# A gated linear-attention kernel with an MLP behind it: gates of the last eight pairs loaded one token per partition, and a new order table on every engine

## The chip, the cores and the metric

One core of one Trainium2 chip runs the whole program. The metric is the device time of one execution in microseconds. The five engines are named as in the profile: PE (TensorE matmuls, with PEld for its weight loads), DVE (VectorE), ACT (ScalarE), POOL (GpSimd) and SP (SyncE, which here only issues DMAs). A "q" behind an engine's name (SPq, ACTq) is its sequencer.

## What is computed

Four batches, eight heads, 768 tokens, 48 channels per head. A complex gate decays a 48x48 state per head; the query reads it; the result of all heads (384 channels) goes through a layer norm and a two-layer MLP with a residual.

```python
mag = sqrt(a_re*a_re + a_im*a_im); scale = minimum(mag, 0.999) / (mag + 1e-06)
for t in range(S):                       # a_re, a_im scaled by `scale`
    S_re, S_im = (ar*S_re - ai*S_im) + k[t] v[t]^T,  ar*S_im + ai*S_re
    y[t] = q[t] @ S_re
x  = y, heads side by side               # (4, 768, 384)
xn = (x - mean) / sqrt(var + 1e-06) * g_ln
out = x + maximum(xn @ w_ch1, 0) @ w_ch2     # 384 -> 1536 -> 384
```

## The kernel before

The 768 tokens of a batch are cut into six chunks of 128, and two chunks make a pair: 12 pairs, P = 0 to 11, chunk n = 2P + c with c = 0 or 1. All work of a pair is made of named steps.

- Loads: `are.P`, `aim.P` (the two parts of the gate), `k.P.c`, `q.P.c`, `vf.P.c`. Each tile has a small ring of buffers (`are`, `aim`, `q`, `k` three, `vf` two), and a load waits until its buffer is free. A gate load of a pair is one DMA of 384 KB: partition p holds the two neighbouring tokens 2p and 2p+1, so that a run of 384 bytes is contiguous in memory (line 445). `k`, `q` and `vf` are loaded one token per partition, in runs of 192 bytes (line 404). Pair 0 is worked in two halves of four heads (`PARTS`), its steps end in `.0.0` and `.0.1`.
- Gate, on ACT, DVE and POOL: `ln` (w = ln a_re), `iv` (1/a_re), `r` = a_im/a_re, `r2`, `u` = ln(1 + r2), `l` and `lc` (log of the magnitude, capped), `th` = arctan r.
- Sums over tokens, on PE: `dec` (line 477) adds up the logs with triangular matrices `u_e`, `ph` (492 and 496) adds up the angles with `u_th` and takes over the carry of the pair before (`car`, through `pick`). Since a partition holds two tokens, each of the two chunks needs the products of both: four 384-column products for `dec`, and four and two with `pick` for `ph`.
- `e`, `en` (exponentials), `sin`, `cos` (with `abs`, or for pairs 0 to 2 a quarter turn `qt`), then `ke`, `qe` (k and q with their decays) and `ks`, `qs` (times cosine and sine).
- Attention within the chunk: `ksT`, `qsT` (transposed by PE as `kT`/`qT` and a copy, or by a DMA from SP), `am` (products), `atm` (mask), `gm` and `G` (state), `y`, `x`. `v` is `vf` in bf16. `dps`, `decc`: the pair's whole decay.
- MLP: `xtr`, `xT` (transposed x), `bn`, `rstd` (layer norm), `mm1` with `relu` (hidden layer, three groups `.P.g` of two parts), `mm2` with `oa` and `ot` (output), `st` (store).
- `warm.i` are fill-ins: products of 256 columns whose result nobody reads, 134 of them, all before the first product of the MLP. `wl` load the weights, `wp` and `wc` fold the layer norm into them. `tab` loads a table of functions on ACT.

The order is written out by hand in one table, `PLAN`: each entry names a step, its engine (P, A, V, G for POOL, S) and, where it needs one, its PSUM bank. Every engine works through its own entries in that order and waits for what a step needs. A load or store with S is issued by SP, one with A by ACT, between ACT's other work. `@name` makes a step wait for the step named, so that POOL and DVE take turns. Which engine does a step is thus decided in the table: `ks:V` on DVE, `ks:G` on POOL.

Of the kernel before, what the change touches and what calls it, by code (L numbers as in the profile page):

```python
# [34 lines left out]

ENGINES = {"P": "PE", "A": "ACT", "V": "DVE", "G": "POOL", "S": "SP"}
# [37 lines left out]
r2.4.0:V mm1.1.0.0:P4 th.4.0:A car.3.0:V0 mm2.0.0:P2 relu.1.0:A4 ke.2.0.1:V mm2.1.0:P3 qs.2.0.1:V vf.2.1:S cos.3.0:A
lc.3.0:V mm2.2.0:P4 qs.2.0.0:V bn.2:V tab.log.6:A qT.4:P5 mm2.1.1:P3 bn.1:V rstd.1:G dec.3.0:P0 ks.2.0.1:V u.4.0:A
ks.2.0.0:V mm2.0.1:P2 rstd.0:G en.3.0:A0 l.4.0:V ksT.5:S mm2.2.1:P4 e.3.0:A0 lc.4.0:V ln.5.0:A relu.1.2:V6
qe.3.0.1:G@lc.4.0 mm2.1.2:P3 qe.3.0.0:G mm2.0.2:P2 aim.5.0:S oa.1:A3 qT.5:P0 iv.5.0:A vf.3.0:A ot.0:V2 dec.4.0:P6
qsT.4:V5 mm2.2.2:P4 e.4.0:A6 vf.3.1:A qs.3.0.1:V kT.4:P1 qs.3.0.0:V en.4.0:A6 dps.3:P5 are.7.0:S dps.4:P2 ksT.4:V1
ke.3.0.0:G@qs.3.0.0 qT.6:P3 qsT.5:A0 ph.4.0:P6 ot.2:V4 aim.6.0:S ke.3.0.1:G ln.6.0:A decc.3:V5 decc.4:V2 am.4:P4
q.4.0:S v.2:G qsT.6:V3 mm2.3.0:P1 iv.6.0:A atm.4:V4 ks.3.0.1:G k.4.0:S qT.7:P2 tab.trig.7:A mm2.3.1:P1 qsT.7:V2  # L80
gm.4:P3 am.5:P4 sin.4.0:A6 ks.3.0.0:V k.4.1:S y.4:P2 atm.5:V4 r.5.0:G@ks.3.0.0 kT.6:P0 car.4.0:A6 mm2.3.2:P1 x.4:A2
G.4:A3 ksT.6:V0 k.5.1:S kT.7:P5 abs.4.0:A6 xtr.4:P4 ot.1:G y.5:P0 ksT.7:V5 q.4.1:S th.5.0:A am.6:P6 x.5:V0 v.3:G
k.5.0:S am.7:P2 xT.4:A4 atm.6:V6 xtr.5:P0 ph.5.0:P4 r2.5.0:G xT.5:A0 cos.4.0:A ot.3:V1 gm.6:P0 mm1.2.1.1:P6 atm.7:V2
G.6:A0 vf.4.1:A r.6.0:G aim.7.0:S abs.5.0:A4 y.6:P1 mm1.2.1.0:P6 x.6:V1 sin.5.0:A4 vf.4.0:A mm1.2.2.1:P2 relu.2.1:V6
cos.5.0:A xtr.6:P1 r2.6.0:G y.7:P4 mm1.2.2.0:P2 th.6.0:A st.0:A x.7:V4 gm.7:P0 bn.7:V xtr.7:P4 tab.log.8:A ke.4.0.1:G
mm1.2.0.0:P6 xT.6:V1 mm1.2.0.1:P6 q.5.1:S xT.7:V4 qe.4.0.0:G G.7:V0 u.5.0:A are.8.0:S mm1.3.0.1:P4 bn.6:V ke.4.0.0:G
mm1.3.0.0:P4 relu.2.2:A2 st.2:A relu.2.0:V6 qe.4.0.1:G mm1.3.1.1:P0 relu.3.0:A4 ks.4.0.0:V mm1.3.2.1:P2 rstd.3:G
ks.4.0.1:V u.6.0:A mm1.3.2.0:P2 l.5.0:V ksT.8:S mm2.5.0:P6 qs.4.0.1:V ln.7.0:A mm1.3.1.0:P0 lc.5.0:V q.5.0:S
qs.4.0.0:V kT.9:P7 relu.3.1:A0 l.6.0:V dec.5.0:P4 qsT.9:S mm2.5.1:P6 iv.7.0:A lc.6.0:V ksT.9:V7 mm2.6.0:P0 en.5.0:A4
q.6.0:S r.7.0:V mm2.4.0:P1 e.5.0:A4 qT.8:P7 q.7.0:S bn.5:V v.4:A r2.7.0:G@r.7.0 dec.6.0:P4 are.9.0:S bn.4:V  # L90
relu.3.2:A2 mm2.4.1:P1 k.6.0:S qsT.8:V7 mm2.6.1:P0 rstd.2:G en.6.0:A4 qe.5.0.1:V am.8:P2 ke.5.0.0:V e.6.0:A4
mm2.4.2:P1 qe.5.0.0:V ln.8.0:A atm.8:V2 gm.8:P7 ke.5.0.1:G@qe.5.0.0 q.6.1:S am.9:P4 iv.8.0:A mm2.6.2:P0 qe.6.0.0:G
atm.9:V4 u.7.0:A st.1:A mm2.5.2:P6 ph.6.0:P2 G.8:A7 vf.6.0:A ks.5.0.1:V k.6.1:S tab.trig.9:A qs.5.0.1:V mm2.7.0:P4
ot.4:V1 abs.6.0:V2 y.8:P5 th.7.0:A vf.5.1:A mm2.7.1:P4 l.7.0:V x.8:A5 vf.5.0:A gm.9:P7 y.9:P1 sin.6.0:A2 vf.6.1:A
mm2.7.2:P4 x.9:V1 car.6.0:A2 xtr.8:P5 qs.5.0.0:V xtr.9:P1 oa.7:A4 ph.7.0:P2 xT.9:V1 qsT.10:S ks.5.0.0:G@qs.5.0.0
xT.8:V5 cos.6.0:A ot.5:V6 qT.11:P1 G.9:V7 sin.7.0:A2 mm1.4.1.0:P4 qe.6.0.1:V abs.7.0:A2 st.4:A mm1.4.1.1:P4 ksT.10:S
qs.6.0.0:V mm1.4.0.1:P6 tab.log.10:A car.7.0:V2 ke.6.0.1:G@qs.6.0.0 mm1.4.0.0:P6 qsT.11:V1 mm1.4.2.0:P2 ln.9.0:A
# [116 lines left out]
def kernel(  # L214
# [12 lines left out]
    nc = tc.nc  # L227
# [596 lines left out]
```

## Time and profile before

| | |
|---|---|
| median of 3 runs | 191.19 us (191.16 to 192.15) |
| the profiled execution, its own time | 192.75 us |
| the profiled execution, span from first to last instruction | 191.0 us |
| instructions | 5154 |
| DMA packets, bytes | 133080, 37.57 MB |
| read from HBM, written | 28.31 MB, 4.72 MB |
| share of the chain that ended last | PE 63%, DVE 10%, ACT 9%, DMA 8%, issue 4% |

The page's busy shares are averages over the whole span; the view by windows gives them for a stretch of time. The mean time of one matmul in the groups holds its latency, since matmuls are pipelined; the time that one really takes of PE is the distance between starts, which the pieces of the chain show (so many products in so many microseconds). The "DMA share" of a window is the packets' time over that of 16 engines; packets of two queues overlap on an engine, so it can exceed 1.

### The profile page before, as it was taken

What the parts mean: (1) busy time and instruction counts of PE and PEld (TensorE: products, weight loads), DVE (VectorE), ACT (ScalarE), POOL (GpSimd) and SP (SyncE); (2) the same over time, 40 slices, a digit from 0 to 9 for tenths busy, and PEclk for the clock granted to TensorE, in tenths of its full rate; (3) what the DMA queues carried; (4) which work ended last, traced back from release to release, by engine and by line L of the source; (5) the groups of instructions that cost most, each with busy time, mean ns of one, the idle gap of its engine ahead of it and who ended that gap; (6) DMA issues with size and microseconds to landing.
All of it is one profiled execution on the core that took longest, in us unless ns stands there. A gap on an engine that the chain in (4) does not pass through costs nothing.

```text
span 191.0 us, 5154 instructions
## 1 busy us (share of the span) xinstructions
PE 177.3 (93%) x2045; PEld 138.6 (73%) x2045; DVE 156.6 (82%) x285; ACT 158.9 (83%) x224; POOL 105.5 (55%) x124
## 2 busy tenths in 40 slices
PE   5999398999999999999968999999999999998992
PEld 3888365788667887776847687877867777786781
DVE  1678699999999999999996998998989867666532
ACT  3989499999999997899949999998999979662340
POOL 7419032579196899071539483347785954940130
PEclk9999999999999999999999999999999999999998
DMA  6999999999969999889999999999799979994032
GB/s 153 278 240 202 212 198 204 210 214 207 242 108 287 205 220 234 154 183 234 136 265 234 190 221 230 282 223 204 141 160 262 217 126 179 256 191 151 5 124 82
DMA packets 133080, 37.57 MB, mean 197 GB/s; under 512 B 127168, under 2 KB 133056, under 8 KB 133056
## 3 DMA queue, kind: packets, MB, share of 16 engines
q1 hardware_dynamic: 107760, 27.21, 70.6%
q10 hardware_dynamic: 22512, 7.67, 18.0%
q0 software_dynamic: 2784, 2.36, 7.9%
q8 instruction: 16, 0.26, 0.6%
q14 instruction: 8, 0.07, 0.1%
HBM read 28.31 MB, written 4.72 MB: 173 GB/s over the span
## 4 chain that ended last, share of the span: by engine, by line
PE 63%; DVE 10%; ACT 9%; DMA 8%; issue 4%; ACTq 2%; POOL 1%; SPq 1%; DVEq 0%; POOLq 0%
PE banks L754 22%; PE banks L722 16%; PE banks L617 5%; PE banks L594 4%; DMA q<-in_q_dram 4%; DMA ksT<-ks 3%; PE banks L477 3%; PE banks L667 2%; ACTq L777 2%; PE banks L496 2%; PE banks L670 2%; DVE w1b L388 2%; DMA are<-in_a_re_dram 2%; PE banks L645 2%; PE banks L688 2%
## 5 line engine op out<-in xcount | busy, mean ns | idle before, releaser
L754 PE MATMUL banks<-w2b,h 128*128 128x384 bf16 (+1 forms) x300 | 55.7, 319 | 0.6 <-ACT h L739 0.6
L722 PE MATMUL banks<-xT,w1b 128*128 128x256 bf16 x432 | 50.9, 272 | 0.7 <-ACT h L739 0.5
L722 PEld LDWEIGHTS <-w1b 128*128 128x128 bf16 x432 | 41.4, 98 | 7.0 <-issue 1.2
L754 PEld LDWEIGHTS <-h 128*128 128x128 bf16 x300 | 26.7, 97 | 13.8 <-ACT h L739 1.0
L295 DVE TENSOR_TENSOR atm<-banks,mask 128x1024 bf16<-128x1024 f32 x24 | 29.0, 1219 | 3.8 <-PE banks L617 2.9
L739 ACT ACTIVATE h<-banks 128x1024 bf16<-128x1024 f32 (+1 forms) x26 | 25.7, 1009 | 4.6 <-DVE ks L295 2.6
L792 ACT ACT_TABLE_LOAD x19 | 24.4, 1283 | 2.6 <-PEq L808 1.3
L295 POOL TENSOR_TENSOR ke<-k,en 128x384 bf16<-128x384 f32 x17 | 15.4, 916 | 14.1 <-ACT e L481 4.3
L767 POOL TENSOR_TENSOR ot<-ot,x 128x384 f32<-128x384 f32 x13 | 12.5, 967 | 14.2 <-ACT ot L760 12.9
L295 POOL TENSOR_TENSOR r<-aim,are 128x768 f16<-128x768 f32 (+1 forms) x8 | 13.7, 1715 | 11.0 <-DVE w1b L388 4.1
L787 PE MATMUL banks<-u_e 128*128 128x256 f16 x134 | 17.5, 286 | 2.2 <-POOL u_e L323 2.2
L295 POOL TENSOR_TENSOR qs<-qe,trig 128x768 bf16<-128x768 bf16 x8 | 13.0, 1640 | 10.3 <-DVE w1b L388 7.2
L617 PE MATMUL banks<-qsT,ksT 128*128 128x128 bf16 x192 | 14.5, 219 | 2.8 <-ACT h L739 2.1
L787 PEld LDWEIGHTS <-u_e 128*128 128x128 f16 x134 | 13.5, 102 | 4.5 <-POOL u_e L323 1.9
L617 PEld LDWEIGHTS <-ksT 128*128 128x128 bf16 x192 | 12.1, 97 | 5.1 <-issue 2.8
L741 DVE TENSOR_SCALAR h<-banks 128x1024 bf16<-128x1024 f32 (+1 forms) x11 | 12.7, 1166 | 2.7 <-PE banks L722 2.7
L295 POOL TENSOR_TENSOR qe<-q,e 128x384 bf16<-128x384 f32 x12 | 11.0, 917 | 6.8 <-DVE r L295 3.6
L466 DVE SCALAR_TENSOR_TENSOR l<-r,w 128x768 f16<-128x768 f16 (+1 forms) x13 | 12.6, 969 | 1.3 <-ACT r L462 1.1
L680 DVE BATCH_NORM_STATS2 stats<-x 128x6 f32<-128x384 bf16 x24 | 13.1, 546 | 0.1
L667 PE MATMUL banks<-v,atm 128*128 128x48 bf16 x192 | 12.0, 183 | 0.0
L514 ACT ACTIVATE trig<-banks 128x768 bf16<-128x768 int16 (+1 forms) x13 | 9.8, 761 | 2.5 <-DVE car L509 2.4
L496 PE MATMUL banks<-th,u_th 128*128 128x384 f16 (+1 forms) x52 | 11.8, 313 | 0.0
(93 smaller groups left out, 380.8 us busy)
## 6 DMA issues: line engine op xcount, KB each, us to landing
k<-in_k_dram SPq DMA_DIRECT2D x24, 192.0 KB, 5.1
q<-in_q_dram SPq DMA_DIRECT2D x24, 192.0 KB, 4.3
are<-in_a_re_dram SPq DMA_DIRECT2D x11, 384.0 KB, 5.1
aim<-in_a_im_dram SPq DMA_DIRECT2D x11, 384.0 KB, 5.0
out_dram<-ot ACTq DMA_DIRECT2D x19, 192.0 KB, 3.4
vf<-in_v_dram ACTq DMA_DIRECT2D x18, 192.0 KB, 4.3
w1b<-in_moe_w_ch_dram POOLq DMA_DIRECT2D x3, 384.0 KB, 7.6
vf<-in_v_dram SPq DMA_DIRECT2D x6, 192.0 KB, 7.0
```

What stands on the lines that cost most here:

```text
L295: {"DVE": nc.vector, "POOL": nc.gpsimd}[eng(name)].tensor_tensor(**kw)
L466: nc.vector.scalar_tensor_tensor(out=S_("l"), in0=S_("r2"), scalar=0.5, in1=S_("w"), op0=ALU.mult, op1=ALU.add)
L496: nc.tensor.matmul(heads(ps[:, c]), lhsT=u_th[:, c, j], rhs=step(T("th", P), j), start=False, stop=(j == R - 1), skip_group_check=True)
L617: nc.tensor.matmul(ps[:, h], lhsT=T("ksT", n)[:, h], rhs=T("qsT", n)[:, h], start=True, stop=True)
L667: nc.tensor.matmul(ps[:, h], lhsT=T("atm", n)[:, h], rhs=T("v", P)[:, c, h], start=True, stop=nfirst)
L680: nc.vector.bn_stats(out=T("stats", n), in_=T("x", n))
L722: nc.tensor.matmul(ps[:, jj], lhsT=w1b[:, dc, ts(gi * JG + jj, C)], rhs=T("xT", P)[:, dc].rearrange("p c t -> p (c t)"), start=(dc == 0), ...
L739: act(out=dst, in_=src, func=AF.Relu)
L741: nc.vector.tensor_scalar(out=dst, in0=src, scalar1=0.0, scalar2=None, op0=ALU.max)
L754: nc.tensor.matmul(bank(own)[:, 0:w], lhsT=T("h", P)[:, j, ts(c, C)], rhs=w2b[:, j, es], start=(j == 0), stop=(j == NJ - 1))
L787: g.add(f"warm.{i}", lambda i=i: nc.tensor.matmul(bank(f"warm.{i}")[:, 0:256], lhsT=u_e[:, 0, 0], rhs=u_e[:, 1].rearrange("p j t -> p (j t ...
L792: g.add(f"tab.{nm}.{i}", lambda tab=tab: nc.scalar.preload_act_table_set(tab))
```

## The change

For pairs 4 to 11 (`NATURAL`) the gates are loaded as `k` and `q` are, one token per partition: two DMAs of 192 KB with 192-byte runs for each of `are` and `aim` (steps `are.P.0.c`, `aim.P.0.c`), in place of one of 384 KB with 384-byte runs. A chunk's running sum then needs its own chunk's triangular product, and for the second chunk one more with a matrix of ones: three products for `dec` in place of four, and five for `ph` in place of six. `ne` (POOL) and `nth` (DVE) make the two new matrices.

```diff
+NATURAL = {4, 5, 6, 7, 8, 9, 10, 11}
...
+            def sums(c, step_t, nat_t, nat=nat):
+                if nat:
+                    return [(nat_t[:, 0 if j == c else 1], j) for j in range(c + 1)]
+                return [(step_t[:, c, j], j) for j in range(R)]
...
+                if nat:
+                    for c in range(R):
+                        add(f"{nm}.{X}.{c}", lambda nm=nm, ap=ap, X=X, c=c, step=step: ring(
+                            f"{nm}.{X}.{c}").dma_start(out=step(T(nm, P), c), in_=ap[b].rearrange(
+                                "h (c p) d -> p c h d", p=C)[:, pp * R + c]), uses=[(nm, P)])
...
-                    for j in range(R):
-                        nc.tensor.matmul(heads(ps[:, c]), lhsT=u_e[:, c, j], rhs=step(T("l", P), j),
-                                         start=(j == 0), stop=(j == R - 1))
+                    parts = sums(c, u_e, n_e)
+                    for i, (lhsT, j) in enumerate(parts):
+                        nc.tensor.matmul(heads(ps[:, c]), lhsT=lhsT, rhs=step(T("l", P), j),
+                                         start=(i == 0), stop=(i == len(parts) - 1))
...
-    for i in range(134):
+    for i in range(114):
```

`PLAN` is replaced as a whole: every engine's order is new, and many steps change their engine. Counted over the two tables (before, after):

| step | before | after |
|---|---|---|
| `warm` on PE | 134 | 114 |
| `kT`, `qT`, `xtr` on PE | 10, 13, 24 | 12, 13, 23 |
| `ksT`, `qsT`, `xT` by DMA from SP | 14, 11, 0 | 12, 11, 1 |
| `x` on ACT / DVE | 12 / 12 | 18 / 6 |
| `G` on ACT / DVE | 8 / 12 | 4 / 16 |
| `abs` on ACT / DVE | 8 / 1 | 4 / 5 |
| `xT` on ACT / DVE | 8 / 16 | 10 / 13 |
| `ot` on POOL (with `oa` on ACT) / DVE | 13 / 12 | 10 / 15 |
| `rstd` on ACT / POOL | 5 / 7 | 10 / 2 |
| `relu` on ACT / DVE | 26 / 11 | 27 / 10 |
| `ks` on DVE / POOL | 21 / 5 | 15 / 11 |
| `qs` on DVE / POOL | 18 / 8 | 19 / 7 |
| `qe` on DVE / POOL | 12 / 12 | 4 / 20 |
| `ke` on DVE / POOL | 7 / 17 | 8 / 16 |
| `r` on DVE / POOL | 5 / 8 | 4 / 9 |
| `r2` on ACT / DVE / POOL | 4 / 4 / 5 | 5 / 5 / 3 |
| `v` on ACT / DVE / POOL | 4 / 3 / 5 | 2 / 1 / 9 |
| gate loads issued by SP / ACT | 24 / 2 | 34 / 8 |
| `k` and `q` issued by SP / ACT | 48 / 0 | 39 / 9 |
| `vf` issued by SP / ACT | 6 / 18 | 17 / 7 |
| `st` issued by SP / ACT | 6 / 19 | 16 / 9 |
| DMAs issued by SP / ACT | 110 / 39 | 131 / 33 |

The pieces of the new table that the prediction speaks of, other engines' entries left out:

```text
ACT:  e.4.0 en.4.0 aim.6.0.1 ln.6.0 vf.2.0 iv.6.0 abs.4.0 tab cos.4.0 sin.4.0 th.6.0 vf.3.1 car.4.0 oa.2 x.4 th.5.0
POOL: ... r.6.0 v.2 r.5.0 r2.6.0 v.3 qe.4.0.1 ke.4.0.1 ...
SP:   ... qsT.9 ksT.8 st.1 aim.7.0.0 st.2 vf.5.0 k.5.0 ...
SP:   ... k.11.1 k.11.0 st.11 vf.11.1 qsT.23 xT.21 vf.11.0 st.14 qsT.22 st.13 ksT.22 ksT.23 ...
```

More of the change, by code (lines that the diff above doesn't have):

```diff
@@ L74 @@
[L74 to L83, printed above, removed]
@@ L94 @@
[L94 to L97, printed above, removed]
-lc.7.0:V aim.8.0:S v.5:V mm1.4.2.1:P2 relu.4.1:A4 st.3:A relu.4.0:V6 qs.6.0.1:G@v.5 kT.11:P1 relu.4.2:A2 aim.9.0:S
```

237 lines of the change are left out of this document (135 added, 102 removed).

## The prediction

> **What bounds the kernel now.** First the page's busy times, then the view by windows, which cuts the span where the MLP's products begin (36 us) and where the attention ends (160 us).
>
> ```profile
> PE 177.3 (93%) x2045; PEld 138.6 (73%) x2045; DVE 156.6 (82%) x285; ACT 158.9 (83%) x224; POOL 105.5 (55%) x124
> ```
>
> ```profile
> core 0: us, PE busy (x) PEld busy (x) DVE busy (x) ACT busy (x) POOL busy (x), PEclk, DMA share, GB/s
> 0.00:36.00 36.00, 29.64 (x298) 23.08 (x298) 26.64 (x51) 29.41 (x45) 15.77 (x37) 1.00 1.00 211
> 36.00:160.00 124.00, 121.08 (x1452) 95.30 (x1451) 112.91 (x206) 115.54 (x155) 79.59 (x78) 1.00 1.06 209
> 160.00:191.00 31.00, 26.57 (x299) 20.19 (x296) 17.01 (x30) 13.98 (x27) 10.12 (x10) 0.97 0.59 133
> ```
>
> The middle stage has no single bound. In 124 us PE idles for 2.9 us, ACT for 8.5, DVE for 11.1, and the DMA engines are full (1.06). POOL alone has room, 44 us. In the first 36 us most of PE's work is fill-ins, and the real work waits for a chain through ACT, DVE and the loads. In the last 31 us ACT and DVE are half idle: there PE's own list sets the end.
>
> So a saving on PE counts in full only in the last stage; in the middle it counts as far as ACT's list, which has 93% of that stage, shrinks with it.
>
> **What PE saves.** The real price of a product is the distance between starts, from pieces of the chain that ended last:
>
> ```profile
> 45.16 4.58 PE banks L722 x42
> 53.04 0.65 PE banks L477 x4
> 58.21 0.45 PE banks L594 x8
> 44.79 0.37 PE banks L688 x6
> ```
>
> Products of 256 columns cost 4.58/42 = 0.109 us, of 384 columns 0.65/4 = 0.163, eight transposes 0.45, three 0.18. The change takes one product of 384 columns from `dec` and one from `ph` in eight pairs: 16 x 0.163 = -2.6 us. Two more transposed chunks on PE cost +0.9, one `xtr` less -0.2: together -1.9 us, all behind the first product of the MLP. The 20 fill-ins (20 x 0.109 = 2.2 us) stood in time in which PE waited, so I cost them at nothing; their cover is the chain of the first stage, and were it gone they would be worth up to those 2.2 us.
>
> **What ACT saves.** ACT's moved steps, one of each:
>
> ```profile
> L290 ACT CAST G<-banks 128x384 bf16<-128x384 f32 x8 | 3.8, 480 | 0.0
> L531 ACT ACTIVATE sh<-banks 128x768 f16<-128x768 int16 x8 | 6.5, 814 | 0.0
> L290 ACT CAST x<-banks 128x384 bf16<-128x384 f32 x12 | 5.7, 477 | 2.5 <-PE banks L670 2.5
> L290 ACT COPY xT<-banks 128x384 bf16<-128x384 bf16 x8 | 3.8, 481 | 5.2 <-PE banks L688 5.2
> L760 ACT ACTIVATE ot<-banks,rstd 128x384 f32<-128x384 f32 x13 | 7.4, 579 | 0.8 <-PE banks L754 0.7
> L705 ACT ACTIVATE rstd<-rstd 128x2 f32<-128x2 f32 x5 | 1.0, 203 | 0.2
> L412 ACT CAST v<-vf 128x768 bf16<-128x768 f32 x4 | 3.3, 835 | 0.0
> L792 ACT ACT_TABLE_LOAD x19 | 24.4, 1283 | 2.6 <-PEq L808 1.3 <-issue 0.9
> L458 ACT ACTIVATE r<-r 128x768 f16<-128x768 f16 x2 | 1.7, 838 | 0.2 <-issue 0.2
> L290 ACT COPY qsT<-banks 128x1024 bf16<-128x1024 bf16 x2 | 2.1, 1028 | 0.0
> ```
>
> I count both tables up to ACT's last `relu` of pair 9, the end of the middle stage. `G` goes from 8 to 2 (-2.9), `abs` from 8 to 4 (-3.3), `qsT` from 2 to 1 (-1.0), `v` from 3 to 2 (-0.8); `rstd` goes from 1 to 8, each two passes of 0.2 (+2.8), `x` from 11 to 15 (+1.9), `xT` from 6 to 8 (+1.0), `r2` from 4 to 5 (+0.8), `oa` from 7 to 8 (+0.6). The sum is -0.9 us, within a stage of 124. I take -0.9 for the middle stage and keep 0 (`rstd`, 0.2 us a pass, hides in waits or not) and -1.9 (PE alone decides) as ends. DVE loses about 6 us to the same point, nearly all `qe` and `ks` that go to POOL; it is not what ends last.
>
> **What POOL takes over.**
>
> ```profile
> L295 POOL TENSOR_TENSOR ks<-ke,trig 128x768 bf16<-128x768 bf16 x5 | 8.2, 1639 | 5.3 <-DVE qs L295 5.1
> L295 POOL TENSOR_TENSOR qe<-q,e 128x384 bf16<-128x384 f32 x12 | 11.0, 917 | 6.8 <-DVE r L295 3.6 <-DVE qe L295 1.6 <-DVE w1b L388 1.1
> L295 DVE TENSOR_TENSOR ks<-ke,trig 128x768 bf16<-128x768 bf16 x17 | 9.0, 550 | 0.8 <-POOL ke L295 0.6
> L295 POOL TENSOR_TENSOR r<-aim,are 128x768 f16<-128x768 f32 x7 | 12.7, 1817 | 8.2 <-DVE w1b L388 4.1 <-DVE stats L680 2.1 <-DVE l L469 1.3
> ```
>
> Six more `ks` (+9.8) and eight more `qe` (+7.3), less `rstd`, `ot` and `r2`: about +9 us of 105.5. That fits into its idle time, but a `ks` that waits for its turn is 1.1 us later on POOL than on DVE.
>
> **What the DMAs take.** The gates of eight pairs are 16 x 384 KB = 6.3 MB, the same bytes in twice the packets, 16,384 more. No view splits packets by size, so I compare two stretches in which the engines are full: at 120 to 124 us mostly gate loads in runs of 384 bytes are under way, at 88 to 92 us `k`, `q` and `vf` in runs of 192.
>
> ```profile
> 88.00:92.00 4.00, 4.00 (x64) 2.95 (x63) 3.90 (x8) 3.94 (x7) 0.19 (x1) 1.00 1.07 215
> 120.00:124.00 4.00, 4.00 (x37) 3.40 (x36) 3.86 (x10) 4.00 (x7) 1.79 (x2) 1.00 1.13 298
> q1 hardware_dynamic: 107760, 27.21, 70.6%
> ```
>
> 6.3 MB at 298 GB/s take 21 us, at 215 GB/s 29 us: +8 us of all 16 engines, 1 us a pair. The ends are 0 (bytes alone count) and 16,384 x 20.0 ns / 16 = +20 us (packets alone count; 20.0 ns is the queue's 70.6% of 16 x 191 us over its 107760 packets). Two DMA transposes fewer give some 2 back. The Trainium skill ("DMA: Bandwidth & Descriptors", Specifications) puts the smallest transfer at line rate at 512 bytes; by that rule both runs are too short and the price lies nearer to the upper end, while the two rows show a difference that is well below it.
>
> Whether this shows depends on how early the loads are. Before, hardly anything waited for one:
>
> ```profile
> DVE qe L295 <- DMA q<-in_q_dram: 2.3, 2, 1.5
> DVE v L414 <- DMA vf<-in_v_dram: 2.3, 1, 2.3
> ACT w L448 <- DMA are<-in_a_re_dram: 1.6, 1, 1.6
> aim<-in_a_im_dram SPq DMA_DIRECT2D x11, 384.0 KB, 5.0
> aim<-in_a_im_dram ACTq DMA_DIRECT2D x2, 192.0 KB, 4.0
> vf<-in_v_dram ACTq DMA_DIRECT2D x18, 192.0 KB, 4.3
> ksT<-ks SPq DMA_TRANSPOSE x14, 4.7
> ```
>
> In the new table some loads are issued close ahead of their use. The plainest: ACT issues `aim.6.0.1`, then does `ln`, `iv`, `abs`, a table load (1.283), `cos`, `sin` and wants `th.6.0`. At the rows' 0.8 to 0.85 us a step (`sh` and `r` above; `ln`, `iv`, `cos` and `sin` have the same 768 columns) that is 5.5 us of work, while the load (4.0 to 5.0 us) and `r.6.0` on POOL (1.8) take 5.8 to 6.8. ACT waits 0.3 to 1.3 us. Behind `r.6.0` POOL has `v.2`, which `y.4` needs, then `r.5.0` and `v.3`, whose half `vf.3.1` ACT issues only after `th.6.0`. I take +0.7 for this place and leave further ones to the rival below.
>
> **The first stage.** It holds one large wait, ACT's `sin.0.0`, which stood behind DVE's `qe` and so behind the load of `q.0.0`:
>
> ```profile
> 13.77 7.08 DMA q<-in_q_dram
> ```
>
> ```profile
> 18.33 1.67 ACT L485 ACTIVATE th<-r 128x384 f16<-128x384 f16 x3
> 22.39 0.87 ACT L514 ACTIVATE trig<-banks 128x384 bf16<-128x384 int16 x2 [2.39 <-DVE car L509]
> ```
>
> The new table puts `qe.0` on POOL and asks SP for `q.1` earlier, so that up to 2.4 us can go and `sin.0.0` starts at 20. But `vf.0.0` now stands on ACT behind `en.2.0`, some 6 us of ACT's list later, at about 26 us: with 4.3 us to land and 0.9 for `v.0` on POOL, `gm.0` and `y.0` follow at about 32 to 33, and ACT stands ahead of `G.0` and `x.0` again. I take -0.2, with -2.4 and +1.0 as ends.
>
> **The last stage.** PE's list behind pair 9's hidden layer is 0.6 us shorter (it is part of the 1.9; the middle stage was costed by ACT, so it counts here). Against it, `xT.21` goes by DMA. At the prices above, PE's list behind `y.21` is 22 us long and that from `mm1.10.0` on 18. So `x.21` is done about 21 us before the end, SP issues behind `qsT.23` at some 20.5, and the tile lands between 1.8 us (three eighths of a `ksT`'s 4.7 for three of its eight blocks, an estimate) and 4.7 us later, for a step due at 18: 0 to 2.2 us late. I take +0.6, nearer to the small end since the tile is small.
>
> **Sum**: -0.9 - 0.2 + 0.7 - 0.6 + 0.6 = -0.4 us. The profiled execution took 192.75 us, 1.75 around its span of 191.0; it would come to 192.35. That execution is 1.56 above the median of 191.19, so against the median I forecast 190.8. Half a per cent (0.96 us) is about what a measurement here can tell from no change, the runs before being 0.99 apart.
>
> **The rivals.**
> *PE decides after all* (24%): ACT's idle time in the middle goes largely to waits for PE and DVE, both of which get relief:
>
> ```profile
> ACT h L739 <- DVE ks L295: 2.6, 1, 2.6
> ACT x L290 <- PE banks L670: 2.5, 3, 1.0
> ACT h L739 <- PE banks L722: 1.8, 3, 0.9
> ```
>
> Then -1.9 counts whole, the first stage gives -1.5 and the shorter waits of ACT some -0.5: 187.3. For it: PE idles less than ACT there (2.9 against 8.5). Against: nine kinds of step change engine and ACT's list does not shrink.
> *Late loads* (32%): the DMA engines, already full, get 1 us more a pair, and the slack goes. Beside the place above, `aim.7.0.0` stands on SP behind two transposes, `vf.11.0` behind `xT.21`, `aim.8` and `vf.3` on ACT close to their use; each blocks POOL's or DVE's queue, and with it `v` or `r`, for 1 us or so. From three such places on it decides: four give +4, 194.8. For it: DMA share 1.06. Against: waits on loads were about 6 us in all, and most in the first stage.
> *The clock falls* (4%): fill-ins stand in fewer, larger lumps, so PE has longer gaps in the first stage. Before, the clock was 1.00 there, though one wait came near:
>
> ```profile
> PE banks L521 <- ACT trig L514: 2.8, 2, 2.6
> ```
>
> At half clock the real products from 10 to 36 us, some 10 us, would double with about a third of that on the chain: +3, 193.8. The Trainium skill ("TensorE: Matmul & The Clock Gate", Part 1) has the clock halve after an idle window of about 3.4 us; by that rule 2.6 us are too short, and the trace agrees, with 1.00 in that stage.
>
> **How the numbers follow.** My forecast (no more than small change, 189.2 to 192.4) gets 40%, of it 11 faster, 23 the same and 6 slower. With the rivals: faster 24 + 11 = 35%, slower 32 + 4 + 6 = 42%, same 23%. The range goes down to 187.0, just under the first rival, and up to 196.0, which takes in the second with one more place and leaves out the price by packets alone.
>
> **What would show it.** PE's `dec` and `ph` products of 384 columns falling by 16; PE's idle time from 36 to 160 us rising by 1 to 2 us with ACT's unchanged (then ACT held it); no wait on DMA over 2 us after 40 us. If POOL's or DVE's waits for `aim` and `vf` sum to over 4 us after 40 us, the late loads are right; if ACT's idle time falls below 7 us, the first rival. A granted clock under 0.9 before 36 us would be the third. I am wrong altogether if a stage that I hold for unchanged, the weights' loading, moves.

## The result and the profile after

| | before | changed kernel |
|---|---|---|
| median | 191.67 us (191.16 to 194.03, 4 runs) | 208.59 us (207.18 to 210.21, 4 runs) |
| ratio | | 1.0859, 95% interval 1.0727 to 1.0991 |
| profiled execution, span | 191.0 us | 205.6 us |

The change costs 8.6%, some 17 us, far outside the predicted range of 187.0 to 196.0. Some executions of a kernel are longer than its others by one to three per cent; the ratios compare only the shorter ones, of which `table_only` and `three_places_old` had one each and so have no ratio, and the profiles of the kernel before, `gates_only` and `table_only` show longer ones.

The first line of the page of the changed kernel answers to the first line shown of before:

```profile
PE 179.0 (87%) x2022; PEld 138.7 (67%) x2022; DVE 163.8 (80%) x276; ACT 157.7 (77%) x230; POOL 114.3 (56%) x128
```

ACT has 1.2 us less to do, as its list promised, and POOL 8.8 us more. DVE, which was to lose 6 us, is busy 7.2 us longer. The view by windows cut at 36 and 160 us, for the stretch that was the middle stage of before:

```profile
core 0: us, PE busy (x) PEld busy (x) DVE busy (x) ACT busy (x) POOL busy (x), PEclk, DMA share, GB/s
36.00:160.00 124.00, 111.11 (x1305) 87.10 (x1303) 107.48 (x179) 102.80 (x149) 73.17 (x66) 0.97 0.96 177
```

PE now idles for 12.9 us of these 124 instead of 2.9, ACT for 21.2 instead of 8.5, DVE for 16.5 instead of 11.1 and POOL for 50.8 instead of 44.4. No engine is as full as before, so the steps wait for each other and for loads: the DMA engines are still busy (0.96 after 1.06), but carry 177 GB/s instead of 209. Finer windows of the same view show where:

```profile
90.00:100.00 10.00, 6.28 (x51) 4.14 (x50) 6.38 (x12) 6.23 (x9) 4.59 (x5) 1.00 1.06 180
...
110.00:120.00 10.00, 6.08 (x77) 5.01 (x75) 5.39 (x13) 5.59 (x9) 7.82 (x8) 0.99 1.34 204
120.00:130.00 10.00, 10.00 (x120) 7.76 (x119) 7.11 (x14) 8.04 (x14) 0.91 (x1) 0.83 1.15 207
130.00:140.00 10.00, 8.20 (x82) 6.28 (x81) 9.97 (x14) 8.73 (x12) 6.52 (x5) 1.00 0.60 136
140.00:150.00 10.00, 9.18 (x120) 7.79 (x120) 8.60 (x18) 6.62 (x11) 2.84 (x3) 0.83 1.00 168
```

Two holes in PE, at 90 to 100 and 110 to 120 us; a stretch in which DVE is full (9.97 of 10) and PE waits, at 130 to 140; and a clock of 0.83 behind two of them. The view of waits (engine, line, what it waited for; us in total, times, longest) names the first partners:

```profile
POOL qe L299 <- DMA q<-in_q_dram: 8.9, 4, 4.9
POOL v L430 <- DMA vf<-in_v_dram: 7.0, 2, 4.2
...
ACT h L774 <- DMA are<-in_a_re_dram: 4.4, 1, 4.4
PE banks L757 <- ACT h L774: 3.9, 1, 3.9
...
ACT x L294 <- DMA k<-in_k_dram: 3.7, 1, 3.7
...
PE banks L723 <- ACT x L294: 3.2, 1, 3.2
...
POOL r L299 <- DMA aim<-in_a_im_dram: 1.2, 1, 1.2
```

The two lines in which ACT waits for a DMA look odd: `h` (a `relu`) and `x` are copies out of PSUM, which use neither `are` nor `k`.

**An account of PE.** To compare kernels I took PE's products from the trace one by one: the distance from a product's start to the next one's, against the usual distance of its kind. "Half clock" is what products cost beyond it whose distance was about twice the usual one, "waits" is all the rest beyond it (all in us, one profiled execution each).

| kernel | products at the usual distance | waits | half clock | ratio to before (95% interval) |
|---|---|---|---|---|
| before | 171.5 | 10.8 | 2.5 | |
| changed | 167.4 | 27.7 | 4.8 | 1.0859 (1.0727 to 1.0991) |
| `gates_only` | 168.5 | 16.6 | 8.0 | 1.0351 (1.0239 to 1.0462) |
| `old_gates_two_loads` | 171.5 | 10.1 | 2.8 | 0.9981 (0.9931 to 1.0031) |
| `gates_one_load` | 168.9 | 14.2 | 6.5 | 1.0213 (1.0088 to 1.0339) |
| `table_only` | 169.6 | 25.8 | 4.5 | none |
| `two_loads_sp` | 167.4 | 23.2 | 4.5 | 1.0639 (1.0591 to 1.0687) |
| `turns` | 167.4 | 24.0 | 3.8 | 1.0587 (1.0511 to 1.0663) |
| `three_places` | 167.4 | 19.8 | 3.9 | 1.0330 (1.0278 to 1.0382) |
| `vg_back` | 167.0 | 35.2 | 4.9 | 1.1308 (1.1233 to 1.1384) |
| `before_st378` | 171.5 | 7.2 | 2.6 | 0.9944 (0.9907 to 0.9982) |

The change took 4.1 us of products from PE (2.2 of fill-ins, 1.9 of real work) and gave back 16.9 us of waits and 2.3 us of half clock. Of the half clock 1.2 us before and 2.4 after are fill-ins of the first 8 us; 2.2 us after lie in two stretches from 120 and from 141 us on, where the kernel before has only single products. By stretches of each kernel's own time the waits are 5.9 us before and 10.7 after (0 to 60 us), 3.2 and 4.4 (60 to 100), 0.1 and 8.0 (100 to 140), 1.6 and 4.6 (from 140 on).

### The profile page after: what moved, and what is told of

The parts are those of the page before. It is cut to its first block, busy times and chain, and to the rows that moved or that the text cites. A ratio compares the mean times of both kernels' runs of the same rounds, so it can differ in the third digit from the quotient of the medians.

```text
span 205.6 us, 5126 instructions
## 1 busy us (share of the span) xinstructions
PE 179.0 (87%) x2022; PEld 138.7 (67%) x2022; DVE 163.8 (80%) x276; ACT 157.7 (77%) x230; POOL 114.3 (56%) x128
## 5 line engine op out<-in xcount | busy, mean ns | idle before, releaser
L757 PE MATMUL banks<-xT,w1b 128*128 128x256 bf16 x432 | 52.2, 276 | 5.5 <-ACT h L774 3.9
L789 PEld LDWEIGHTS <-h 128*128 128x128 bf16 x300 | 26.8, 98 | 13.3 <-ACT h L774 0.6
L774 ACT ACTIVATE h<-banks 128x1024 bf16<-128x1024 f32 (+1 forms) x27 | 26.7, 1007 | 10.3 <-PE banks L757 5.6
L299 POOL TENSOR_TENSOR qe<-q,e 128x384 bf16<-128x384 f32 x20 | 18.5, 935 | 20.1 <-DMA q<-in_q_dram 8.9
L299 POOL TENSOR_TENSOR ks<-ke,trig 128x768 bf16<-128x768 bf16 x11 | 18.4, 1682 | 9.9 <-DVE ke L299 6.8
L299 POOL TENSOR_TENSOR r<-aim,are 128x768 f16<-128x768 f32 (+1 forms) x9 | 15.5, 1720 | 8.0 <-ACT are L483 3.6
L294 ACT CAST x<-banks 128x384 bf16<-128x384 f32 x18 | 8.5, 476 | 10.0 <-PE banks L705 5.5
L822 PEld LDWEIGHTS <-u_e 128*128 128x128 f16 x114 | 12.1, 109 | 4.9 <-POOL u_e L329 1.9
L299 DVE TENSOR_TENSOR qs<-qe,trig 128x768 bf16<-128x768 bf16 (+1 forms) x19 | 13.0, 703 | 1.2 <-POOL qe L299 1.0
L776 DVE TENSOR_SCALAR h<-banks 128x1024 bf16<-128x1024 f32 (+1 forms) x10 | 11.5, 1160 | 3.0 <-PE banks L757 2.9
L802 POOL TENSOR_TENSOR ot<-ot,x 128x384 f32<-128x384 f32 x10 | 9.0, 912 | 7.1 <-ACT ot L795 4.8
```

Source lines behind the costliest of these rows:

```text
L299: {"DVE": nc.vector, "POOL": nc.gpsimd}[eng(name)].tensor_tensor(**kw)
L757: nc.tensor.matmul(ps[:, jj], lhsT=w1b[:, dc, ts(gi * JG + jj, C)], rhs=T("xT", P)[:, dc].rearrange("p c t -> p (c t)"), start=(dc == 0), ...
L774: act(out=dst, in_=src, func=AF.Relu)
L776: nc.vector.tensor_scalar(out=dst, in0=src, scalar1=0.0, scalar2=None, op0=ALU.max)
L789: nc.tensor.matmul(bank(own)[:, 0:w], lhsT=T("h", P)[:, j, ts(c, C)], rhs=w2b[:, j, es], start=(j == 0), stop=(j == NJ - 1))
L802: nc.gpsimd.tensor_tensor(out=T("ot", n)[:, es], in0=T("ot", n)[:, es], in1=T("x", n)[:, es], op=ALU.add)
```

## The experiments

### Gate layout or order table

The change has two parts that can be had apart. `gates_only` keeps the old table and only splits its gate loads in place; `table_only` keeps the old gates in the new table.

```diff
-aim.4.0:S
+aim.4.0.0:S aim.4.0.1:S
```

```diff
-NATURAL = {4, 5, 6, 7, 8, 9, 10, 11}
+NATURAL = set()
...
-are.4.0.1:S ... are.4.0.0:S
+are.4.0:S
```

> The old order table with the new gate layout alone: gates of pairs 4 to 11 in two half loads each, 3 and 5 sum products, 134 fill-ins. If the 14 to 17 us come from the new table (theory), this takes 188.5 to 192.5 us: 2.6 us of PE products fewer, of which the middle stage passes little on, and DMA engines that carry the doubled packets without a wait. If the half loads are the cause (rival: twice the packets and twice the issues fill the DMA engines), this alone takes over 197 us and the waits on are and aim grow by several us.

> The new order table with the old gate layout: each gate in one load (at the place and on the queue of its first half), 4 and 6 sum products; the two steps that make the triangle of ones stay. Theory (the table is the cause): 203 to 211 us, with ACT idle for several us in one piece somewhere behind a load that it issues itself. Rival (half loads): under 196 us.

Measured: 198.32 us (196.0 to 202.32), ratio 1.0351 (1.0239 to 1.0462), for the gates alone, and 207.41 us (204.06 to 207.58) for the table alone. Neither theory had it whole: each part costs by itself, the gates 2.4 to 4.6% and the table some 13 us in its one shorter execution (204.06 us) and 16 to 17 in the others (207.3 to 207.6). The two together, some 17 us, cost less than the parts in sum (some 7 and 13 or more). At pair 3's `relu.3.0` the profiled execution of `gates_only` (201.34 us) is 1.8 us behind that of before (78.5 us against 76.7), at pair 7's `relu.7.0` 9.6 us (146.9 against 137.3): the loss comes in the stretch in which the DMA engines were full already.

### Why the gate layout costs: the number of loads or the short runs

At first I held the number of loads for the cause. In the trace the DMAs of SP and ACT share eight semaphores, and an issue comes only when the last DMA of its semaphore has landed; the new layout has 16 loads more to issue. Four kernels on the old table: the old layout in two loads a gate; runs of 192 bytes in one load a gate (it computes with other tokens' gates, at the same work and bytes); `gates_only` with ACT's `vf` loads and stores issued by SP; and the kernel before with ACT's `vf` loads and `st.3` issued by SP.

```diff
-    out=T(nm, P)[:, hs], in_=ap[b][hs].rearrange("h (k p j) d -> p k h (j d)", p=C, j=R)[:, pp])
+    out=T(nm, P)[:, ch], in_=ap[b][ch].rearrange("h (k p j) d -> p k h (j d)", p=C, j=R)[:, pp])   # ch: heads 0-3, 4-7
```

```diff
-    out=step(T(nm, P), c), in_=ap[b].rearrange("h (c p) d -> p c h d", p=C)[:, pp * R + c])
+    out=T(nm, P).rearrange("p h (j d) -> p (h j) d", d=D),
+    in_=ap[b].rearrange("h (c p) d -> p (h c) d", p=C)[:, ds(pp * R, H * R)])
```

```diff
-vf.3.0:A ... st.0:A
+vf.3.0:S ... st.0:S
```

> The kernel before with each gate of pairs 4 to 11 loaded in two loads of four heads each: the runs stay 384 bytes, the packets and sums are those of before, only 16 more loads are issued. Theory slots (the gate change costs time because every load takes one of a few places under way, and an engine whose load finds none stands): 195 to 200 us, like the 198.3 of the old table with the new gate layout, with ACT standing behind vf and st that it issues. Rival packets (the runs of 192 bytes cost it): 190 to 192.

> The old table with 3 and 5 sum products and each gate of pairs 4 to 11 in one load of 16 runs of 192 bytes. The 16 runs are taken from neighbouring chunks, so that one load can describe them, and the gates are other tokens' ones; work and bytes are the same. Theory slots: 188 to 191.5 us, no more than before. Rival packets: 196 to 200, with waits on are and aim.

> The old table with the new gate layout, and the 37 vf loads and stores that ACT issues up to relu.11.0 issued by SP at the same place. Theory slots: ACT no longer stands behind them, the time falls from 198.3 to 189 to 194 us. Rival (the DMA engines themselves are the limit): 196 to 200, the same data come as late as before.

> The kernel before with ACT's vf loads and st.3 issued by SP at the same place. If ACT's standing behind st.3 at 99 us (2.3 us of PE) is a cost of the same kind, the time falls by 1 to 3 us, to 187.5 to 190. Rival: SP, which has the transposes too, stands in turn and a load comes late: 190 to 194.

Measured: 191.66 us (ratio 0.9981, 0.9931 to 1.0031), 198.21 (1.0213, 1.0088 to 1.0339), 200.28 (1.0415, 1.0336 to 1.0494) and 191.21 (0.9896, 0.9820 to 0.9972). My theory of the number fell and its rival is left: twice the loads with the old runs cost nothing, the same number of loads with runs of 192 bytes costs 1 to 3%. (Whether the doubled number adds to that where the runs are short, 3.5% against 2.1%, the intervals don't say.) The queue line of the page (packets, MB, the packets' time as a share of 16 engines) of `old_gates_two_loads` and of `gates_one_load` prices the runs:

```profile
q1 hardware_dynamic: 108016, 27.21, 72.2%
```

```profile
q1 hardware_dynamic: 124144, 27.21, 75.6%
```

72.2% of 190.6 us and 75.6% of 195.9 us are 137.6 and 148.1 us of all 16 engines, for the same bytes: the short runs take 10.5 us more (13.3 against the kernel before). SP, which issues these loads, is held up too: summed over its DMAs behind 40 us, its issues take 94.5 us before, 99.5 with two loads a gate and 109.5 with one load in short runs. How that reaches PE shows in the timeline of ACT in `gates_one_load` (start, us, step; in brackets the idle time before it):

```profile
88.13 0.81 ACT L547 ACTIVATE trig<-banks 128x768 bf16<-128x768 int16 x1
93.02 0.38 ACTq L419 DMA_DIRECT2D vf<-in_v_dram  x1
93.44 0.48 ACT L539 ACTIVATE car<-banks 32x384 f16<-32x384 int16 x1 [4.50 <-DMA k<-in_k_dram]
```

ACT stood for 4.5 us in front of its own issue of `vf.6.1`, until `k.6.1`, the last load of the same semaphore, had landed at 93.00; PE, waiting for `car`, stood as long. In the kernel before `k.6.1` landed at 90.84 and `vf.6.1` went out at 89.82, on another semaphore. So the loads land later, but which loads share a semaphore has changed too, though their number has not; no run parts the two, and half clock behind PE's two longest stalls adds 3.8 us in this trace. That the short runs cost by themselves is argued from `gates_only_sp` as well: with ACT's `vf` loads and stores issued by SP the new layout is 4.2% slower than before, while `before_sp`, the old layout with ACT's `vf` loads and `st.3` on SP, is faster than before by 0.3 to 1.8%. The price is then not in ACT's issues alone, though SP has more stores to issue in the first of the two. Where `gates_only_sp` pays it was not followed to PE: POOL's `ke` waits 6.5 us for `k` there, but 4.1 us in `before_sp` too.

### Why the new table costs: loads that ACT issues

> The changed kernel with the 19 loads that ACT issues behind vf.0.0 issued by SP at the same place of the table. Theory A (a load that waits for its turn stops ACT's arithmetic behind it): the pieces of 3.7 and 4.4 us in which ACT stood before k.5.1 and are.11.0.0 are gone, PE's stalls of 3.4 us at 90 us and 4.1 us at 115 us too, and the time falls by 5 to 9 us, to 198.5 to 203.5. Rival (the loads are late wherever they are issued): the same steps wait for the same data, the time stays within 2 us of 208, and the waits show as DMA k, q or are on POOL, DVE or ACT.

```diff
-k.5.1:A ... are.11.0.0:A        (19 loads behind vf.0.0)
+k.5.1:S ... are.11.0.0:S
```

Measured: 204.58 us (ratio 1.0699, 1.0605 to 1.0792). That is 4.0 us below the median of the changed kernel, less than expected, and its interval still overlaps that one's. PE's two stalls were gone, but a new one of 2.6 us had come at 174 us, where SP issued a store late and ACT's `ot` waited for its buffer. The sharper test moves only the two loads in front of which ACT stood longest. The timeline of ACT in the changed kernel:

```profile
89.53 0.46 ACT L294 CAST x<-banks 128x384 bf16<-128x384 f32 x1
93.31 0.37 ACTq L420 DMA_DIRECT2D k<-in_k_dram  x1
93.73 0.48 ACT L294 CAST x<-banks 128x384 bf16<-128x384 f32 x1 [3.74 <-DMA k<-in_k_dram]
...
112.75 1.51 ACT L549 ACTIVATE trig<-banks 128x768 bf16<-128x768 int16 x2
118.16 0.38 ACTq L474 DMA_DIRECT2D are<-in_a_re_dram  x1
118.64 1.02 ACT L774 ACTIVATE h<-banks 128x1024 bf16<-128x1024 f32 x1 [4.38 <-DMA are<-in_a_re_dram]
```

The ACTq rows explain the odd waits. `x.9` waits for no data: between `x.8` and `x.9` the table has the load `k.5.1`, whose issue came at 93.31, 0.02 us after `k.6.1` of the same semaphore had landed (93.29). Before `relu.5.0` stands `are.11.0.0`, issued at 118.16, 0.02 us after `are.10.0.0` (118.14).

```diff
-k.5.1:A ... are.11.0.0:A
+k.5.1:S ... are.11.0.0:S
```

> The changed kernel with two tokens changed: k.5.1 and are.11.0.0 issued by SP instead of ACT at the same place. Theory A (ACT's arithmetic stands behind these two issues): PE's stalls of 3.4 us at 90.7 and 4.1 us at 115.6 shrink to under 1 us each, relu.6.0 ends 4 to 7 us earlier than 134.2, and the time falls by 3 to 7 us, to 202 to 206. Rival (the steps behind wait for something else that is as late): under 1.5 us.

Measured: 203.34 us, ratio 1.0639 (1.0591 to 1.0687), clear of the changed kernel's interval. The same place in the timeline of ACT, both `x` now in one piece:

```profile
88.88 0.84 ACT L491 ACTIVATE r<-r 128x768 f16<-128x768 f16 x1
89.63 0.85 ACT L294 CAST x<-banks 128x384 bf16<-128x384 f32 x2
90.38 0.85 ACT L495 ACTIVATE r<-r 128x768 f16<-128x768 f16 x1
```

Two tokens of the table are worth 5.3 us between the medians (the two ratios lie 2.2% apart, give or take 1.4%). PE's stalls of 3.4 and 4.1 us are gone, pair 6's `relu` ends at 129.5 instead of 134.2 us, and the half clock has left 120 to 130 us (the trace shows it at 103 to 107 instead, behind other short stalls).

### Why the new table costs: DVE beside POOL

> The changed kernel with six early steps put back from POOL on DVE (qs.0.0.0, qs.0.0.1, ke.1.0.1, ks.1.0.1, qs.2.0.0, qs.2.0.1), and qe.2.0.0 on POOL made to wait for ks.1.0.0 on DVE. Theory B (DVE's SBUF steps stretch while POOL computes): DVE's ks and qs of 2.58 and 1.51 us come back to about 0.55, x.1 ends at 36 to 37 us instead of 39.0, and the time falls by 1.5 to 4 us, to 204 to 207. Rival (the first stage is late because vf.0.0 is loaded later): x.1 stays at 39 and the time within 1 us of 208.

```diff
-qs.0.0.1:G ... qs.0.0.0:G ... ke.1.0.1:G ... ks.1.0.1:G@qs.1.0.1 ... qe.2.0.0:G ... qs.2.0.0:G ... qs.2.0.1:G
+qs.0.0.1:V ... qs.0.0.0:V ... ke.1.0.1:V ... ks.1.0.1:V ... qe.2.0.0:G@ks.1.0.0 ... qs.2.0.0:V ... qs.2.0.1:V
```

Measured: 206.06 us, ratio 1.0762 (1.0669 to 1.0856), which overlaps the changed kernel's: by the time alone it is not told apart. The trace tells it: `x.1` ends at 37.2 us instead of 39.0 (36.5 before). DVE's timeline of the changed kernel, then of `first_dve`:

```profile
34.02 1.51 DVE L299 TENSOR_TENSOR qs<-qe,trig 128x768 bf16<-128x768 bf16 x1
35.45 2.58 DVE L299 TENSOR_TENSOR ks<-ke,trig 128x768 bf16<-128x768 bf16 x1
```

```profile
35.25 0.54 DVE L299 TENSOR_TENSOR qs<-qe,trig 128x768 bf16<-128x768 bf16 x1
35.71 0.55 DVE L299 TENSOR_TENSOR ks<-ke,trig 128x768 bf16<-128x768 bf16 x1
```

The same steps take 0.55 us alone and 1.5 to 2.6 us beside POOL. The plainest place is at 135 us (the changed kernel's timeline, DVE, then POOL):

```profile
135.16 2.09 DVE L299 TENSOR_TENSOR ke<-k,en 128x384 bf16<-128x384 f32 x1
137.18 2.46 DVE L299 TENSOR_TENSOR qs<-qe,trig 128x768 bf16<-128x768 bf16 x2
139.56 1.21 DVE L299 TENSOR_TENSOR atm<-banks,mask 128x1024 bf16<-128x1024 f32 x1
...
135.02 1.82 POOL L299 TENSOR_TENSOR r<-aim,are 128x768 f16<-128x768 f32 x1 [0.73 <-ACT are L483]
137.40 3.73 POOL L299 TENSOR_TENSOR ks<-ke,trig 128x768 bf16<-128x768 bf16 x2 [0.56 <-DVE ke L299]
```

DVE's `ke` starts 0.14 us after POOL's `r` and ends 0.41 us after it (137.25 against 136.84), so it seems to have stood for nearly all of `r` (alone, in `turns` below, `ke` takes 0.64 us). The Trainium skill ("SBUF — State Buffer", section "SBUF: two separate sides") says that DVE and GpSimd share a pair of ports that one of them holds for a whole instruction while the other is blocked, also where the DVE step has two SBUF inputs; by that rule `ke` had to wait for the end of `r`, and the trace agrees to within some 0.2 us. Summed over the span, DVE's steps take 4.0 us beyond their usual length in the kernel before and 13.7 us in the changed one.

`vg_back`, `vg_back_sp` and `vg_back_sp_old` were to take that away wholesale, by putting the 52 elementwise steps that changed between DVE and POOL back on their old engines.

```diff
-qs.0.0.1:G ... ks.5.0.0:V ... (52 steps)
+qs.0.0.1:V ... ks.5.0.0:G@qs.5.0.0 ...
```

> The changed kernel with the 52 elementwise steps (r, ke, qe, ks, qs, v) that the new table moved between DVE and POOL back on the engine they had before, at the new table's places. Theory B (DVE's steps stretch beside POOL's): the time that DVE's steps take beyond their usual length falls from 13.7 us to under 7, PE's stall of 2.8 us at 138 us goes, x.1 ends by 37.5, and the time falls by 4 to 7 us, to 201 to 205. Rival (the places in the table, not the engines, cost it): 206 to 210.

> The same, and the 19 loads that ACT issues behind vf.0.0 issued by SP. If theory A (4.0 us alone) and theory B add up: 197 to 202. If both act on the same waits: 201 to 205.

> The same as vg_back_sp with the old gate layout (one load a gate in runs of 384 bytes, 4 and 6 sum products). What the packets cost shows against vg_back_sp: 5 to 8 us by the old table's 7.5 (then 191 to 196), about 1 us by the new table's 1.2. What remains above 192 belongs to the places of the new table alone: loads close ahead of their use and the order on each engine.

Measured: 214.9 us (1.1308, 1.1233 to 1.1384), 215.81 (1.1312, 1.1206 to 1.1419) and 219.3 (1.1495, 1.1368 to 1.1621): all slower than the changed kernel. They did not do what they were made for: DVE's stretch rose to 20.1, 19.4 and 18.4 us, for the steps that went to POOL fell beside DVE's again, and in `vg_back` PE stood 6.0 us in one piece at 107 us. These three tell nothing on the theory. The last test therefore moves no work at all. It only makes POOL wait.

```diff
-qe.8.0.1:G@qs.7.0.1 ... ke.8.0.1:V ... r.10.0:G ... qs.8.0.1:V
+ke.8.0.1:V qe.8.0.1:G@ke.8.0.1 ... qs.8.0.1:V r.10.0:G@qs.8.0.1
```

> The changed kernel with three POOL steps told to wait: qe.8.0.1, and with it qe.8.0.0, behind ke.8.0.1 on DVE, and r.10.0 behind qs.8.0.1 on DVE. No step changes its engine. Theory B (DVE's ke and qs stretch from 0.55 to 1.2 to 2.1 us while POOL computes beside them): ke.8 and qs.8 come back to 0.55 each, atm.15 starts about 3 us earlier than 139.6, PE's stall of 2.8 us at 138 us falls under 1, and the time falls by 1.5 to 4 us, to 204.5 to 207. Rival (two more waits only cost): 208.5 to 211, the stall stays.

Measured: 203.36 us, ratio 1.0587 (1.0511 to 1.0663), clear of the changed kernel's interval. DVE's timeline, and POOL's, in `turns`:

```profile
133.99 0.64 DVE L299 TENSOR_TENSOR ke<-k,en 128x384 bf16<-128x384 f32 x1
134.55 1.01 DVE L299 TENSOR_TENSOR qs<-qe,trig 128x768 bf16<-128x768 bf16 x2
135.49 1.21 DVE L299 TENSOR_TENSOR atm<-banks,mask 128x1024 bf16<-128x1024 f32 x1
...
135.70 1.81 POOL L299 TENSOR_TENSOR r<-aim,are 128x768 f16<-128x768 f32 x1 [1.49 <-ACT h L774]
```

`ke` and `qs` are back at 0.64 and 0.5 us each, `atm.15` starts 4.1 us earlier, and PE's stall of 2.8 us at 138 us is gone, and the half clock behind it: two added waits are worth 5 us.

### Do they add up

```diff
+  the edits of first_dve and turns
-k.5.1:A ... are.11.0.0:A ... q.6.1:A ... q.7.0:A ... vf.6.1:A
+k.5.1:S ... are.11.0.0:S ... q.6.1:S ... q.7.0:S ... vf.6.1:S
```

> The changed kernel with the edits of first_dve and turns, and five loads of ACT issued by SP (k.5.1, are.11.0.0, q.6.1, q.7.0, vf.6.1: all in front of which ACT stood until a transfer landed). If the three causes add up: 208.6 - 2.5 (first stage) - 4 to 6 (loads) - 1.5 to 4 (turns) = 196 to 200.6. If each only uncovers the next wait: 202 to 206.

> The same with the old gate layout: one load a gate in runs of 384 bytes, 4 and 6 sum products. If the short runs cost time wherever nothing else is later: 2 to 6 us below three_places. If the new table hides them: within 1.5 us of it.

Measured: 198.3 us, ratio 1.0330 (1.0278 to 1.0382), for `three_places`, and 203.84 (200.35 to 204.32) for it with the old gates. The first came out where the parts in sum were expected. Some ten of the seventeen microseconds are found: 5 for ACT's issues, 5 for the overlap in pair 8, while what the first stage's edits add is within the scatter. The old gates bring the new table nothing (200.35 us at the lowest); there the price of the short runs does not show. Of the 9.0 us of waits by which `three_places` still exceeds before, 4.6 lie in the first 60 us and 3.6 behind 140 us (10.5 and 5.2 against 5.9 and 1.6); their causes were not tried one by one, and so some seven of the seventeen microseconds stay open.

### Does the kernel before pay for the same thing

The prediction quoted ACT's `h` as waiting 2.6 us for DVE's `ks`. With the ACTq row beside it the timeline of the kernel before reads otherwise:

```profile
96.17 1.01 ACT L739 ACTIVATE h<-banks 128x1024 bf16<-128x1024 f32 x1
99.28 0.36 ACTq L777 DMA_DIRECT2D out_dram<-ot  x1
99.74 1.02 ACT L739 ACTIVATE h<-banks 128x1024 bf16<-128x1024 f32 x1 [2.57 <-DVE ks L295]
```

ACT stood in front of the store `st.3`, which went out 0.02 us after `ksT.10`, a transpose on the same semaphore, had landed (99.25). Three kernels move such stores to SP.

```diff
-st.3:A
+st.3:S
```

```diff
-st.3:A ... st.7:A ... st.8:A     (before_sp_st78: and the 18 vf loads)
+st.3:S ... st.7:S ... st.8:S
```

> The kernel before with one token changed: st.3 issued by SP instead of ACT. If ACT's standing behind st.3 (2.3 us of PE at 98 us) counts in full, 188 to 190; if it only moves on, 190.5 to 192.

> The kernel before with three tokens changed: st.3, st.7 and st.8 issued by SP instead of ACT at the same place. If ACT's standing behind st.3 (PE 2.3 us at 98 us) and st.8 (1.9 us at 127 us) are both gone: 187.5 to 190, faster than before by 1 to 3 us. Rival: SP, which issues without a pause there, brings k.9 and q.9 later, and the wait comes back as one for k: within 0.5% of before.

> The same with ACT's vf loads on SP too (before_sp, 1.0% faster than before, with st.7 and st.8 on SP besides). If ACT's issues are the cost: 187 to 190. If SP's queue is the limit: 190 to 193, with POOL waiting for k as in before_sp, 4.1 us.

Measured: 191.24 us (0.9996, 0.9951 to 1.0042), 189.93 (0.9944, 0.9907 to 0.9982) and 191.12 (0.9967, 0.9922 to 1.0011). With `st.3` alone the wait moved on: ACT then stood 2.5 us in front of `st.8`, and PE 1.9 us at 128 us. With all three on SP PE's waits fall from 10.8 to 7.2 us and the kernel is faster than before by 0.2 to 0.9%; from `before_st3` the intervals do not tell it apart. Moving the `vf` loads too adds nothing to that.

## Why the prediction was wrong, point by point

- *What PE saves*: right. The products at their usual distance fell by 4.1 us, 2.2 for the fill-ins and the forecast 1.9 of real work. The `dec` and `ph` products fell by 16, as the sign said. It was the only term of weight that came true, and the waits swallowed it.
- *What ACT saves*, -0.9 us: the list did shrink (busy -1.2 us over the span). The step that failed is the reading behind it, "the middle stage was costed by ACT" through its list of arithmetic. ACT's list also holds the DMAs that it issues, and I counted what the change moves among them (`k`, `q` and gate loads from SP to ACT) as places in a table, not as work on ACT's path. Two of them cost about 5 us. Each has no length of its own; its price is when an earlier, unrelated transfer lands.
- *What POOL takes over*: the amount was right, +9 us forecast and +8.8 measured; that it "fits into its idle time" was the error. I asked whether POOL had room and not what DVE does meanwhile. DVE's steps lengthened by 9.7 us in sum, more than its list lost, so that DVE was busy 7.2 us longer; at one place of pair 8, undoing the overlap gave back 5 us. The `ks` "1.1 us later on POOL" was the wrong price for it.
- *What the DMAs take*: +8 us of 16 engines was a fair size (10.5 to 13.3 measured, inside the ends of 0 and 20). The error is that the sum entered it at nothing, although the engines were full (share 1.06 to 1.13). On the old table the layout costs 2.4 to 4.6%, and runs of 192 bytes without more loads 1 to 3%; in the one stall followed to its end a load that landed 2.2 us later held up an issue of ACT, and with it PE for 4.5 us. The Trainium skill ("DMA: Bandwidth & Descriptors", Specifications) has transfers under 512 bytes fall short of line rate; the two queue lines agree that 192 bytes cost more than 384, by half to two thirds of the 20 us that a price by packets alone would be.
- *The late place* `aim.6.0.1`, +0.7: the load landed at 63.51 us, 3.9 us after its issue, and `r.6.0` began at 63.72 after a wait of 3.3 us that the profile puts down to DVE's `dec` (its end was at 63.71). ACT did not wait in front of `th.6.0` (66.16). The one wait on `aim` in the view, 1.2 us, is that of `r.7.0` at 86.9. Nothing was lost in that stretch (the changed kernel was 3.8 us behind at `x.5`, and 3.1 us at pair 3's `relu`).
- *The first stage*, -0.2 with ends of -2.4 and +1.0: it lost 2.5 us to `x.1`. The wait behind `q.0.0` did go, as foreseen, but DVE's steps beside POOL's (6.2 us of stretch between 20 and 40 us) took its place; with six steps back on DVE 1.8 us returned. That leaves 0.7 us for all else, the late `vf.0.0`, which I had charged, among it.
- *The last stage*, 0.0 in sum: from pair 9's `relu` to pair 11's it took 23.1 us against 21.4. `xT.21` was right (it landed 2.3 us after its issue, between the two estimates), but `ksT.22`, which SP issues behind it, came late and PE stood 1.3 us.
- *The rivals*: "late loads" was the right family and four times too small. Its sign came (DVE and POOL waited 9.7 us for `aim` and `vf` behind 40 us, where over 4 was to show it; before it was 3.7), but its mechanism, a load that blocks POOL's or DVE's queue for 1 us, was the lesser part: the loads that cost most blocked ACT's queue, and blocked it before they were issued. "PE decides after all" fell with ACT's idle time of 21.2 us. "The clock falls" did not happen where I had put it (1.00 up to 36 us in the view) and did at 0.83 in two later windows, behind stalls, for 2.2 us.
- *"Wrong altogether"*: the weights' loading did move. POOL issued the third load of `w1b` at 27.1 us instead of 18.7, and it landed at 33.5 instead of 27.7. But the first product that reads it (`wp.2`) came at 39.6, so it waited for other things, and this is not what cost the time.

## What to carry to other kernels

A DMA in the list of an engine that also computes can be a wait of unknown length on that engine (here up to 4.5 us): read the issue rows beside the engine's own, and where one stands out a landing, move that one token before anything else. When work goes from DVE to POOL, ask not only whether POOL has room but which DVE step with two SBUF inputs will run beside it; a wait that keeps them apart can be worth more than the work moved. And a price on a resource that is full already, here the DMA engines, must not enter the sum at nothing.

## What the runs showed of the hardware that was not expected

- A stall shorter than 3 us can cost the clock. The stall of 2.78 us at 138 us was followed by half clock up to 143.8, in the windows of the changed kernel:

```profile
138.00:141.00 3.00, 0.38 (x11) 0.29 (x8) 3.00 (x3) 0.73 (x2) 3.00 (x2) 0.90 0.03 5
141.00:144.00 3.00, 3.00 (x36) 2.59 (x35) 2.97 (x6) 1.88 (x4) 0.93 (x2) 0.54 1.00 187
```

  The one of 3.39 us at 90.7 us left it at 1.00, and the one of 4.06 us at 115.6 us did not (0.83 in the window behind it). The Trainium skill ("TensorE: Matmul & The Clock Gate", Part 1) has the clock halve after an idle window of about 3.4 us that runs freely; the second and third agree with that, the first is too short for it, and the measurement decides. The trace's record of the granted clock shows what the three have in common: it is 0.5 from 119.89 to 123.31 us and from 140.37 to 143.79, 3.41 us each time, and the two starts lie six such steps apart. Cut into these steps, the stall of 2.78 us leaves PE idle for 2.2 us of the one from 136.96 to 140.37, and that of 4.06 us for 3.2 of the one before 119.89; that of 3.39 us falls half and half into two, 1.5 and 1.7 us. In all twenty traces of this case, cut the same way, each step with 2.0 us idle or more was followed by one at half clock, and each step at full clock with 1.9 or less by one at full clock. So the idle time within a step counted here, and where the steps fall is luck: the first full clock came at 4.9 us in the kernel before and at 6.8 in `before_st3`, which begins alike.
- Of the DMAs that SP and ACT issue, each takes one of eight semaphores in the trace, and several issues came exactly 0.02 us after the last DMA on the same one had landed. In the changed kernel and the kernel before none of the 164 and 149 issues came earlier than that. Which DMAs share one changed in `before_st3`, where one store went to another engine, and in `gates_one_load`, where no load was added, so an edit far off can put a new wait on ACT; it may be part of the 2.1% of `gates_one_load`.
